# Cached attention beside a gated MLP, one token: MLP products behind the first K units, a longer loop on PE, and a re-ordered last head

## The chip, the cores and the metric

The kernel runs on one core of one Trainium2 chip. Its time is the device time of one execution in microseconds; three runs gave 2554.81, 2555.20 and 2555.25 us, a median of 2555.2. The engines are named PE (matrix products), DVE (vector), ACT (activation), POOL and SP (which issues the loads here). One execution was also recorded by the profiler.

## The reference

One token x (512 values) goes two ways, and a gate mixes them:

```python
g = sigmoid((x * gate_w).sum(-1, keepdims=True))
q = (x @ wq).reshape(B, Sq, H, Dh).transpose(0, 2, 1, 3)       # H = 32, Dh = 128
scores = einsum("bhqd,bhkd->bhqk", q, k_cache) * Dh ** -0.5    # Sk = 65536
o = einsum("bhqk,bhkd->bhqd", softmax(scores), v_cache)
a = o.transpose(0, 2, 1, 3).reshape(B, Sq, H * Dh) @ wo        # 512 columns
b = (silu(x @ w_gate) * (x @ w_up)) @ w_down                   # F = 1792
out = g * a + (1 - g) * b
```

All inputs are bf16. K and V of one head have 65536 rows of 128 values, 16.8 MB each; over 32 heads the two caches make up nearly all the bytes that are read.

## The kernel before

**Places and the order of loads.** SBUF holds a ring of four places (NPL = 4) of 4 MB. K and V of a head are four places each: k(h,0) to k(h,3), v(h,0) to v(h,3). `plan_stream` (L25) writes out the order of the loads: first wq, k(0,0), w_gate with w_up, w_down, then the other seven K places of heads 0 and 1; then, for heads 2 to 31, k(h,t) and v(h-2,t) in turn ("steady", 240 places); then the V places of heads 30 and 31 ("last"). Load number n goes to place n modulo 4. wo (4 MB) is loaded behind v(30,3) into kt, the buffer of transposed K, once all scores are done. The last place of all, v(31,3), is loaded in three parts of 64, 32 and 32 rows (L73), with a semaphore for each.

**SP** (L170 to L193) issues these loads strictly in order on one queue. Before a load that takes over a place it waits until the former owner has been read: a K place until DVE has transposed it (`ktdone`), a V place until its products are done (`pvdone`), wq until q is computed (`s_q`), w_gate and w_up until their products are done (`s_h`), w_down until its products are done (`s_b`). So k(0,3) takes the place of w_gate and w_up, and k(1,0) that of w_down.

**DVE** (from L264) transposes each K place in two units of 64 rows (L326), u = 0 to 7 in a head, into two buffers in turn; a unit's buffer is free again when the scores of the unit two before it are done. Between the units it does the small steps: the row maximum of the head before (L305), the transpose of its exponentials (L311), the reciprocal of its sum (L315), and, behind unit 4 of head 0, `mlp_steps` (L293 to L301): it waits for the exponential of the gate products (`s_sig`), makes silu(gate) * up (`s_gu`), then waits for the down products (`s_b`) and scales that row.

**PE** (from L347) computes q (L358). `scores(h, t)` (L385) makes 16 products with 512 moving columns for each unit (L396). In head 0, behind unit 3, come the 112 gate and up products (`mlp_up`, L373), and behind unit 4 the 14 down products (`mlp_down`, L381). `values(h, t)` (L406) multiplies a V place with the probabilities: for heads 0 to 30 in 32 products with V moving, 512 columns each, which sum four rows of 512 in psO (L418); for head 31 in 128 products with V stationary and one moving column, which sum one column of 128 (L423). For the former ACT scales the four rows by the reciprocal of the sum (`row_norm`, L225 to L230, into orow), PE turns them into one column with four products (`turn`, L429, L434, float32), and ACT copies the column (`column`, L232 to L234, into oTn). `turn(h-1)` stands behind v(h,1). `project(h)` (L438, L443) adds one head's column times wo to psY.

The order of PE's instructions is the order of the places. The K places of heads 0 and 1 and the first 20 steady places are written out, the next 208 are 13 passes of a hardware loop of 16 places (two heads; every wait shifts by 16 counts a pass), the last 12 steady places and the "last" ones are written out again. Behind v(31,2) PE waits for wo and does 31 wo products (L474 to L476), then v(31,3), and at last `project(31)`.

**The end.** DVE scales the column of head 31 out of psO (L340), PE does project(31), DVE mixes in the MLP row (L343), ACT stores the result (L260).

Of the kernel before, what the change touches and what calls it, by code (L numbers as in the profile page):

```python
# [6 lines left out]
ROWS = 128  # L7
# [3 lines left out]
NPL = 4  # L11
NSEM = 16
STEP = 8

ALU = mybir.AluOpType
ACT = mybir.ActivationFunctionType
# [19 lines left out]
def bass_gated_mix__mha_block_cached__swiglu_ffn__decode_kernel(  # L36
# [30 lines left out]
    for n, item in enumerate(items):  # L67
        s = n % NPL
        if item[0] in "kv":
            place[item] = s  # L70
            parts = [(0, ROWS)]
            if item == ("v", H - 1, PL - 1):
                parts = [(0, 64), (64, 96), (96, 128)]  # L73
            for r0, r1 in parts:
                landed[item + (r1,)] = len(dmas)
                dmas.append((item, r0, r1, s, owner[s]))
        else:
            for j, name in enumerate(item):
                place[name] = (s, j)
                landed[name] = len(dmas)  # L80
                dmas.append(((name,), 0, 0, s, owner[s]))
        owner[s] = item
        if item == ("v", H - 2, PL - 1):
            landed["wo"] = len(dmas)
            dmas.append((("wo",), 0, 0, None, None))

    with ExitStack() as ctx:
# [127 lines left out]
        @block.scalar  # L215
        def _(act):
            act.wait_ge(s_z, 1)
            nc.scalar.activation(sc[0:1, 1:2], sc[0:1, 0:1], ACT.Exp, scale=-1.0).then_inc(s_e1, 1)

            def windows(h):  # L220
                if h >= 2:
                    act.wait_ge(qkdone, UN * (h - 1))
                nc.scalar.copy(qcol[:, h % 2], qd[:, h, :, :]).then_inc(s_qw, STEP)  # L223

            def row_norm(h):  # L225
                act.wait_ge(s_li, h + 1)
                act.wait_ge(pvdone, PL * (h + 1))
                if h >= 1:
                    act.wait_ge(s_pt, h)
                nc.scalar.mul(orow[0:4, :], psO[0:4, h % 2, :], Li[0:4, h:h + 1]).then_inc(s_or, STEP)  # L230

            def column(h):  # L232
                act.wait_ge(s_pt, h + 1)
                nc.scalar.copy(oTn[:, h:h + 1], psT[:, h % 2:h % 2 + 1]).then_inc(s_oc, STEP)  # L234

            act.wait_ge(s_qd, 1)
            act.wait_ge(s_qz, 1)
            windows(0)
            windows(1)
            act.wait_ge(s_h, 1)  # L240
            nc.scalar.activation(hbuf[:, 0, 0:FC], psM[:, 64:64 + FC], ACT.Exp, scale=-1.0).then_inc(s_sig, 1)
            for h in range(H):
                act.wait_ge(s_ar, h + 1)
                nc.scalar.mul(nbias[:, h:h + 1], amx[:, h:h + 1], -SCALE).then_inc(s_nb, 1)  # L244
                act.wait_ge(s_nb, h + 1)
                if h >= 2:
                    act.wait_ge(s_pb, STEP * (h - 1))
                nc.scalar.activation(pa[:, h % 2, :], psS[:, h % 2, :], ACT.Exp, bias=nbias[:, h:h + 1],  # L248
                                     scale=SCALE, accum_out=rsum[:, h:h + 1]).then_inc(expdone, STEP)
                if h + 2 < H:  # L250
                    windows(h + 2)
                if h >= 3:
                    column(h - 3)
                if h >= 2:
                    row_norm(h - 2)
            column(H - 3)
            row_norm(H - 2)
            column(H - 2)
            act.wait_ge(s_fin, 1)
            act.dma_start(out_dram, fin[0:1, :]).then_inc(s_out, 16)  # L260
            act.wait_ge(s_out, 16)

        @block.vector
        def _(dve):  # L264
            chain = [0]

            def link(ins):
# [8 lines left out]
            nc.vector.tensor_tensor_reduce(out=orow[0:1, :], in0=xrow[0:1, :], in1=gwrow[0:1, :],  # L276
                                           scale=1.0, scalar=0.0, op0=ALU.mult, op1=ALU.add,
                                           accum_out=sc[0:1, 0:1]).then_inc(s_z, 1)
            dve.wait_ge(s_xT, 1)
            nc.vector.tensor_copy(xTb[:, 0:Dc], psM[:, 0:Dc]).then_inc(s_xTb, 1)  # L280
            dve.wait_ge(s_e1, 1)
# [11 lines left out]
            def mlp_steps():  # L293
                dve.wait_ge(s_sig, 1)
                link(nc.vector.tensor_scalar_add(hbuf[:, 1, 0:FC], hbuf[:, 0, 0:FC], 1.0))
                link(nc.vector.reciprocal(hbuf[:, 2, 0:FC], hbuf[:, 1, 0:FC]))
                link(nc.vector.tensor_tensor(hbuf[:, 0, 0:FC], psM[:, 64:64 + FC], hbuf[:, 2, 0:FC], ALU.mult))
                nc.vector.tensor_tensor(guT[:, 0:FC], hbuf[:, 0, 0:FC], psM[:, 80:80 + FC],
                                        ALU.mult).then_inc(s_gu, 1)
                dve.wait_ge(s_b, 1)  # L300
                link(nc.vector.tensor_scalar(brow[0:1, :], psY[0:1, :], sc[0:1, 4:5], None, ALU.mult))  # L301

# [14 lines left out]
            for h in range(H):  # L317
                for u in range(UN):
# [5 lines left out]
                    src = ring[:, place[("k", h, u // 2)], (u % 2) * UNIT:(u % 2 + 1) * UNIT]  # L324
                    src = src.bitcast(U32).rearrange("p (r j t) -> p r j t", j=2, t=32)
                    nc.vector.transpose(o, src).then_inc(ktdone, 1)  # L326
                    if i == 4:
                        mlp_steps()
                    if u == 0 and h >= 1:
                        head_max(h - 1)  # L330
                    if u == 1 and h >= 1:
                        head_turn(h - 1)
                    if u == 3 and h >= 1:
# [3 lines left out]
            head_norm(H - 1)  # L337
            dve.wait_ge(s_li, H)
            dve.wait_ge(pvdone, PL * H)
            nc.vector.tensor_scalar(oTn[:, H - 1:H], psO[:, (H - 1) % 2, 0:1], Li[:, H - 1:H], None,  # L340
                                    ALU.mult).then_inc(s_otn, 1)
            dve.wait_ge(s_y, 1)
            nc.vector.scalar_tensor_tensor(out=fin[0:1, :], in0=psY[0:1, :], scalar=sc[0:1, 3:4],  # L343
# [3 lines left out]
        def _(pe):  # L347
# [37 lines left out]
            def scores(h, t, more=0):  # L385
                for u in (2 * t, 2 * t + 1):
# [11 lines left out]
                                                    start=(u == 0 and k == 0 and je == 0),  # L398
                                                    stop=(u == UN - 1 and k == 3 and je == 3))
                    done.then_inc(qkdone, 1)  # L400
                    if h == 0 and u == 3:
                        mlp_up()
                    if h == 0 and u == 4:
                        mlp_down()

            def values(h, t, more=0):  # L406
                if t == 0:
                    pe.wait_ge(s_pb, STEP * (h + 1) + more)
                    if h >= 2:
                        pe.wait_ge(s_or, STEP * (h - 1) + more)  # L410
                v = ring[:, place[("v", h, t)], :]
                ends = [e for e in (64, 96, 128) if ("v", h, t, e) in landed]
                for r in range(0, ROWS, 4):
                    if r == 0 or r in ends:
                        arrived(pe, landed[("v", h, t, min(e for e in ends if e > r))], more)
                    k, rho = 8 * t + r // 16, r % 16
                    if h < H - 1:
                        done = nc.tensor.matmul(psO[0:4, h % 2, :], pbk[:, h % 2, k, rho:rho + 4],  # L418
                                                v[:, r * Dh:(r + 4) * Dh],
                                                start=(t == 0 and r == 0), stop=(t == PL - 1 and r == ROWS - 4))  # L420
                    else:
                        for j in range(4):
                            done = nc.tensor.matmul(psO[:, h % 2, 0:1], v[:, (r + j) * Dh:(r + j + 1) * Dh],  # L423
                                                    pbk[:, h % 2, k, rho + j:rho + j + 1],
                                                    start=(t == 0 and r + j == 0),
                                                    stop=(t == PL - 1 and r + j == ROWS - 1))
                done.then_inc(pvdone, 1)

            def turn(h, more=0):  # L429
                pe.wait_ge(s_or, STEP * (h + 1) + more)  # L430
                if h >= 2:
                    pe.wait_ge(s_oc, STEP * (h - 1) + more)
                for i in range(4):
                    done = nc.tensor.matmul(psT[:, h % 2:h % 2 + 1], orow[0:4, i * Dh:(i + 1) * Dh],  # L434
                                            unit[0:4, i:i + 1], start=(i == 0), stop=(i == 3))
                done.then_inc(s_pt, 1)

            def project(h):  # L438
                if h < H - 1:
                    pe.wait_ge(s_oc, STEP * (H - 1))  # L440
                else:
                    pe.wait_ge(s_otn, 1)
                done = nc.tensor.matmul(psY[0:1, :], oTn[:, h:h + 1], wo_ap[:, h, :],  # L443
# [4 lines left out]
            def run(item, more=0):  # L448
# [2 lines left out]
                    scores(h, t, more)  # L451
                else:
                    values(h, t, more)
                    if t == 1 and h >= 1:
                        turn(h - 1, more)

            pe.wait_ge(s_qd, 1)
            pe.wait_ge(s_unit, 1)
            head, per = 4 + 4 * PL, 4 * PL
            loops = (len(steady) - head) // per  # L460
            for item in first:
                if item[0] == "k":
                    run(item)
            for item in steady[:head]:
                run(item)
            with pe.Fori(0, STEP * 2 * loops, STEP * 2) as more:
                for item in steady[head:head + per]:
                    run(item, more)
            for item in steady[head + per * loops:]:
                run(item)  # L470
            for item in last:
                run(item)
                if item == ("v", H - 1, PL - 2):
                    arrived(pe, landed["wo"])  # L474
                    for h in range(H - 1):
                        project(h)  # L476
            project(H - 1)


# [26 lines left out]
```

## Time and profile before

| what | value |
|---|---|
| median of three runs | 2555.2 us |
| the profiled execution | 2555.05 us |
| its span (first to last instruction) | 2553.3 us |
| bytes read | 1087.64 MB, 426 GB/s over the span |
| PE busy | 2042.0 us (80%) |
| DVE busy | 1168.7 us (46%) |
| ACT, POOL busy | 56.1 us (2%), 26.0 us (1%) |
| transpose of one K unit (L326) | 4426 ns, 256 times |
| granted PE clock, mean | 0.90 |

The profiled execution's time is 1.75 us longer than its span. Busy time of an engine is the time in which its instructions run, waits left out; the products of PE overlap, so that 32 of them with a mean of 379 ns (L418) take 7.07 us together. The page cuts the span into 40 slices of 63.8 us and gives for each the busy tenths, the granted clock and the rate of the transfers.

### The profile page before, as it was taken

What the parts mean: (1) busy time and instruction counts of PE and PEld (TensorE: products, weight loads), DVE (VectorE), ACT (ScalarE), POOL (GpSimd) and SP (SyncE); (2) the same over time, 40 slices, a digit from 0 to 9 for tenths busy, and PEclk for the clock granted to TensorE, in tenths of its full rate; (3) what the DMA queues carried; (4) which work ended last, traced back from release to release, by engine and by line L of the source; (5) the groups of instructions that cost most, each with busy time, mean ns of one, the idle gap of its engine ahead of it and who ended that gap; (6) DMA issues with size and microseconds to landing.
All of it is one profiled execution on the core that took longest, in us unless ns stands there. A gap on an engine that the chain in (4) does not pass through costs nothing.

```text
span 2553.3 us, 19880 instructions
## 1 busy us (share of the span) xinstructions
PE 2042.0 (80%) x8992; PEld 824.2 (32%) x9118; DVE 1168.7 (46%) x373; ACT 56.1 (2%) x193; POOL 26.0 (1%) x75
## 2 busy tenths in 40 slices
PE   4778887887788788878877888887888788888885
PEld 2323333333333333333333333333333333333333
DVE  4754445444544544444454445445444544454420
ACT  0000000000000000000000000000000000000000
POOL 0000000000000000000000000000000000000000
PEclk8899889889988988899889988989888988899996
DMA  8999999999999999999999999999999999999998
GB/s 350 402 434 430 431 431 431 433 431 432 433 430 432 432 432 432 431 433 431 431 432 431 432 432 432 431 431 433 431 432 432 432 431 431 432 432 431 430 429 326
DMA packets 41879, 1088.11 MB, mean 426 GB/s; under 512 B 4211, under 2 KB 8310, under 8 KB 8310
## 3 DMA queue, kind: packets, MB, share of 16 engines
q1 hardware_dynamic: 41844, 1087.65, 99.2%
q8 instruction: 22, 0.36, 0.1%
q14 instruction: 11, 0.09, 0.0%
q10 hardware_dynamic: 2, 0.00, 0.0%
HBM read 1087.64 MB, written 0.00 MB: 426 GB/s over the span
## 4 chain that ended last, share of the span: by engine, by line
DMA 75%; DVE 12%; issue 10%; PE 2%; SPq 0%; DVEq 0%
DMA ring<-in_A_k_cache_dram 72%; DVE kt L326 12%; DMA ring<-in_A_v_cache_dram 3%; PE psS L396 1%; DMA gwrow<-in_gate_w_dram 0%; PE psY L443 0%; SPq L190 0%; PE psO L418 0%; PE psO L423 0%; PE psM L373 0%; PE psM L358 0%; PE psY L381 0%; DVE orow L276 0%; DVE brow L301 0%; DVE fin L343 0%
## 5 line engine op out<-in xcount | busy, mean ns | idle before, releaser
L326 DVE STREAM_TRANSPOSE kt<-ring 128x4096 uint32<-128x4096 uint32 x256 | 1125.6, 4426 | 1255.5 <-DMA ring<-in_A_k_cache_dram 1252.6
L396 PE MATMUL psS<-kt,qw 128*128 128x512 bf16 x3970 | 1104.3, 442 | 463.8 <-DVE kt L326 463.2
L418 PE MATMUL psO<-ring,pb 128*4 128x512 bf16 x3968 | 876.8, 379 | 5.0 <-DMA ring<-in_A_v_cache_dram 5.0
L396 PEld LDWEIGHTS psS<-kt,qw 128*128 128x128 bf16 x4096 | 429.7, 108 | 1124.3 <-issue 388.4
L418 PEld LDWEIGHTS psO<-ring,pb 128*4 128x4 bf16 x3968 | 335.2, 87 | 538.9 <-issue 53.2
L244 ACT ACTIVATE nbias<-amx 128x1 f32<-128x1 f32 x32 | 6.5, 203 | 2338.6 <-POOL amx L211 2338.6
L340 DVE TENSOR_SCALAR oTn<-psO,Li 128x1 bf16<-128x1 f32 x1 | 0.2, 220 | 83.8 <-PE psO L423 83.8
L211 POOL PARTITION_ALL_REDUCE amx<-mxs x32 | 11.2, 351 | 2383.9 <-DVE mxs L305 2383.9
L434 PEld LDWEIGHTS psT<-unit,orow 4*128 4x128 f32 x248 | 30.7, 190 | 13.1 <-issue 13.0
L423 PE MATMUL psO<-pb,ring 128*128 128x1 bf16 x512 | 14.1, 165 | 24.9 <-DMA ring<-in_A_v_cache_dram 24.9
L434 PE MATMUL psT<-unit,orow 4*128 4x1 f32 x248 | 33.3, 251 | 0.0
L311 DVE STREAM_TRANSPOSE pb<-pa 128x512 bf16<-128x512 bf16 x32 | 21.4, 670 | 6.4 <-PE psO L418 6.4
L305 DVE TENSOR_REDUCE mxs<-psS 128x1 f32<-128x512 f32 x32 | 20.9, 653 | 5.8 <-PE psS L396 5.8
L423 PEld LDWEIGHTS psO<-pb,ring 128*128 128x128 bf16 x512 | 13.8, 102 | 26.0 <-issue 15.4
L248 ACT ACTIVATE pa<-psS,nbias 128x512 bf16<-128x512 f32 x32 | 22.0, 687 | 2.9 <-ACT nbias L244 0.4
L230 ACT ACTIVATE orow<-psO,Li 4x512 f32<-4x512 f32 x31 | 20.9, 674 | 23.2 <-PE psO L418 23.2
L213 POOL PARTITION_ALL_REDUCE Lt<-rsum x32 | 12.3, 384 | 38.3 <-ACT pa L248 38.3
L352 PE MATMUL psM<-ones,xrow 1*128 1x1 bf16 x4 | 0.3, 172 | 13.9 <-DMA gwrow<-in_gate_w_dram 13.9
L443 PE MATMUL psY<-kt,oTn 128*1 128x512 bf16 x32 | 10.3, 492 | 0.4 <-DVE oTn L340 0.4
L223 ACT COPY qw<-qd 128x16 bf16<-128x16 bf16 x32 | 7.9, 250 | 6.0 <-DVE qd L289 6.0
L373 PEld LDWEIGHTS psM<-xTb,ring 128*128 128x128 bf16 x112 | 6.9, 159 | 0.2
L373 PE MATMUL psM<-xTb,ring 128*128 128x1 bf16 x112 | 6.8, 198 | 0.0
(39 smaller groups left out, 41.1 us busy)
## 6 DMA issues: line engine op xcount, KB each, us to landing
ring<-in_A_k_cache_dram SPq DMA_DIRECT2D x128, 4096.0 KB, 30.0
ring<-in_A_v_cache_dram SPq DMA_DIRECT2D x127, 4096.0 KB, 28.0
ring<-in_A_wq_dram SPq DMA_DIRECT2D x1, 4096.0 KB, 13.0
kt<-in_A_wo_dram SPq DMA_DIRECT2D x1, 4096.0 KB, 38.4
ring<-in_A_v_cache_dram SPq DMA_DIRECT2D x1, 2048.0 KB, 38.7
ring<-in_A_v_cache_dram SPq DMA_DIRECT2D x2, 1024.0 KB, 41.6
ring<-in_B_w_gate_dram SPq DMA_DIRECT2D x1, 1792.0 KB, 25.9
ring<-in_B_w_up_dram SPq DMA_DIRECT2D x1, 1792.0 KB, 29.6
```

What stands on the lines that cost most here:

```text
L211: nc.gpsimd.partition_all_reduce(amx[:, h:h + 1], mxs[:, h:h + 1], P, RMAX).then_inc(s_ar, 1)
L213: nc.gpsimd.partition_all_reduce(Lt[:, h:h + 1], rsum[:, h:h + 1], P, RADD).then_inc(s_L, 1)
L230: nc.scalar.mul(orow[0:4, :], psO[0:4, h % 2, :], Li[0:4, h:h + 1]).then_inc(s_or, STEP)
L248: nc.scalar.activation(pa[:, h % 2, :], psS[:, h % 2, :], ACT.Exp, bias=nbias[:, h:h + 1], scale=SCALE, accum_out=rsum[:, h:h + 1]).then_i ...
L305: nc.vector.reduce_max(mxs[:, h:h + 1], psS[:, h % 2, :], AX_X).then_inc(s_mx, 1)
L311: nc.vector.transpose(pb[:, h % 2, :], pa[:, h % 2, :]).then_inc(s_pb, STEP)
L326: nc.vector.transpose(o, src).then_inc(ktdone, 1)
L373: done = nc.tensor.matmul(psM[:, o + j:o + j + 1], w[:, c, :, j], xTb[:, c:c + 1], start=(c == 0), stop=(c == Dc - 1))
L396: done = nc.tensor.matmul(psS[:, h % 2, :], qw[:, h % 2, je, at0:at0 + 128], ktb[i % 2][:, je // 2, k, :, je % 2], start=(u == 0 and k == ...
L418: done = nc.tensor.matmul(psO[0:4, h % 2, :], pbk[:, h % 2, k, rho:rho + 4], v[:, r * Dh:(r + 4) * Dh], start=(t == 0 and r == 0), stop=(t ...
L423: done = nc.tensor.matmul(psO[:, h % 2, 0:1], v[:, (r + j) * Dh:(r + j + 1) * Dh], pbk[:, h % 2, k, rho + j:rho + j + 1], start=(t == 0 an ...
L434: done = nc.tensor.matmul(psT[:, h % 2:h % 2 + 1], orow[0:4, i * Dh:(i + 1) * Dh], unit[0:4, i:i + 1], start=(i == 0), stop=(i == 3))
```

## The change

- The MLP's gate and up products move from behind unit 3 of head 0 to behind unit 0, the down products from behind unit 4 to behind unit 1. On DVE `mlp_steps` moves from behind unit 4 to behind unit 1, and its last step is a function of its own, `mlp_row`, behind unit 3.
- PE's loop takes all 240 steady places in 15 passes. So that each pass is alike, the waits on `s_or` and `s_oc` have no exceptions for the first heads; instead DVE sets orow to zero at the start and counts `s_or` up by two heads, ACT counts `s_oc` up by three, and a turn of "head -1" is done behind v(0,1).
- Head 31 uses the products with V moving in its first three places. ACT copies their four rows unscaled, `turn(31)` brings them as a column into psT in front of v(31,3), and the 128 one-column products of v(31,3) add to that column. DVE scales it at the end.
- v(31,3) is loaded in four parts: 64, 32, 16 and 16 rows.
- The wo products of heads 0 to 29 stand behind v(31,0), that of head 30 behind v(31,1).

```diff
+ENDS = (64, 96, 112, 128)
...
-                parts = [(0, 64), (64, 96), (96, 128)]
+                parts = [(a, b) for a, b in zip((0,) + ENDS, ENDS)]
...
             def row_norm(h):
...
-                if h >= 1:
-                    act.wait_ge(s_pt, h)
+                act.wait_ge(s_pt, h + 1)
...
             def column(h):
-                act.wait_ge(s_pt, h + 1)
+                act.wait_ge(s_pt, h + 2)
...
+            act.sem_inc(s_oc, 3 * STEP)
...
             column(H - 2)
+            act.wait_ge(pvdone, PL * H - 1)
+            nc.scalar.copy(orow[0:4, :], psO[0:4, (H - 1) % 2, :]).then_inc(s_or, STEP)
...
+            dve.wait_ge(s_z, 1)
+            nc.vector.memset(orow[:], 0.0).then_inc(s_or, 2 * STEP)
...
+            def mlp_row():
                 dve.wait_ge(s_b, 1)
...
-                    if i == 4:
+                    if i == 1:
                         mlp_steps()
+                    if i == 3:
+                        mlp_row()
...
-            nc.vector.tensor_scalar(oTn[:, H - 1:H], psO[:, (H - 1) % 2, 0:1], Li[:, H - 1:H], None,
+            nc.vector.tensor_scalar(oTn[:, H - 1:H], psT[:, (H - 1) % 2:(H - 1) % 2 + 1], Li[:, H - 1:H], None,
...
-                    if h == 0 and u == 3:
+                    if h == 0 and u == 0:
                         mlp_up()
-                    if h == 0 and u == 4:
+                    if h == 0 and u == 1:
                         mlp_down()
...
-                    if h >= 2:
-                        pe.wait_ge(s_or, STEP * (h - 1) + more)
+                    pe.wait_ge(s_or, STEP * (h + 1) + more)
...
-                    if h < H - 1:
+                    if (h, t) != (H - 1, PL - 1):
...
-                            done = nc.tensor.matmul(psO[:, h % 2, 0:1], v[:, (r + j) * Dh:(r + j + 1) * Dh],
+                            done = nc.tensor.matmul(psT[:, h % 2:h % 2 + 1], v[:, (r + j) * Dh:(r + j + 1) * Dh],
...
             def turn(h, more=0):
-                pe.wait_ge(s_or, STEP * (h + 1) + more)
-                if h >= 2:
-                    pe.wait_ge(s_oc, STEP * (h - 1) + more)
+                pe.wait_ge(s_or, STEP * (h + 3) + more)
+                pe.wait_ge(s_oc, STEP * (h + 2) + more)
...
-                    pe.wait_ge(s_oc, STEP * (H - 1))
+                    pe.wait_ge(s_oc, STEP * (h + 4))
...
-                    if t == 1 and h >= 1:
+                    if t == 1:
                         turn(h - 1, more)
...
-            with pe.Fori(0, STEP * 2 * loops, STEP * 2) as more:
-                for item in steady[head:head + per]:
+            with pe.Fori(0, STEP * 2 * (len(steady) // per), STEP * 2) as more:
+                for item in steady[:per]:
                     run(item, more)
...
+                if item == ("v", H - 1, PL - 1):
+                    turn(H - 1)
                 run(item)
-                if item == ("v", H - 1, PL - 2):
+                if item == ("v", H - 1, 0):
                     arrived(pe, landed["wo"])
-                    for h in range(H - 1):
+                    for h in range(H - 2):
                         project(h)
+                if item == ("v", H - 1, 1):
+                    project(H - 2)
             project(H - 1)
```

## The prediction

> **What bounds the kernel now.** I read the page's slices first: is any stretch not bound by transfers?
>
> ```profile
> DMA  8999999999999999999999999999999999999998
> GB/s 350 402 434 430 431 431 431 433 431 432 433 430 432 432 432 432 431 433 431 431 432 431 432 432 432 431 431 433 431 432 432 432 431 431 432 432 431 430 429 326
> ```
>
> From the third slice to the last but one the DMA engines are full at about 432 GB/s, and the page's first line has 1088.11 MB in all: at 432 that is 2518.8 us of the 2553.3 us span. So 34.5 us are missing from the stream, nearly all in the first two slices and the last (a little in the transfer of wo). PE is busy 80%, DVE 46%; in the middle a faster engine buys nothing. The change must be priced at the two ends.
>
> At the start, the view by stretches of 4 us shows the gap (columns: stretch, length, busy time and instructions of each engine, granted PE clock, DMA share, GB/s):
>
> ```profile
> 48.00:52.00 4.00, 1.12 (x3) 0.42 (x4) 4.00 (x2) 0.00 (x0) 0.00 (x0) 0.50 1.07 459
> 52.00:56.00 4.00, 4.00 (x14) 1.49 (x13) 3.14 (x1) 0.00 (x0) 0.00 (x0) 0.69 0.44 188
> 56.00:60.00 4.00, 3.94 (x22) 1.84 (x21) 3.56 (x1) 0.00 (x0) 0.00 (x0) 1.00 0.02 4
> 60.00:64.00 4.00, 4.00 (x70) 4.00 (x69) 0.89 (x1) 0.00 (x0) 0.00 (x0) 1.00 0.00 0
> 64.00:68.00 4.00, 3.75 (x47) 3.04 (x48) 0.76 (x4) 0.18 (x1) 0.00 (x0) 0.59 0.39 106
> 68.00:72.00 4.00, 4.00 (x11) 1.38 (x10) 0.00 (x0) 0.00 (x0) 0.00 (x0) 0.56 0.73 311
> ```
>
> The queue is empty from about 54.5 to 67. Why, say the waits of SP's queue in the first 130 us:
>
> ```profile
> SPq L190 <- PE psM L373: 33.7, 1, 33.7
> SPq L190 <- PE psY L381: 8.8, 1, 8.8
> ```
>
> SP issues in order. After k(0,2) at about 32.6 it stands 33.7 us at the load of k(0,3), whose slot holds w_gate and w_up until the MLP's first products (L373, s_h) end at 66.6; meanwhile everything issued lands. It then waits for the down products (L381, s_b) to load k(1,0).
>
> At the end, the timeline:
>
> ```profile
> 2514.07 3.56 PE L423 MATMUL psO<-pb,ring 128*128 128x1 bf16 x128 [14.51 <-DMA ring<-in_A_v_cache_dram]
> 2533.43 3.57 PE L423 MATMUL psO<-pb,ring 128*128 128x1 bf16 x128 [4.36 <-DMA ring<-in_A_v_cache_dram]
> 2536.93 9.73 PE L443 MATMUL psY<-kt,oTn 128*1 128x512 bf16 x31
> 2546.59 3.37 PE L423 MATMUL psO<-pb,ring 128*128 128x1 bf16 x128
> 2550.07 0.22 DVE L340 TENSOR_SCALAR oTn<-psO,Li 128x1 bf16<-128x1 f32 x1 [83.75 <-PE psO L423]
> ```
>
> PE waits for the first place of the last V, but the last place starts without a wait: 31 wo products stand before it. In stretches of 1 us the last bytes land at about 2542.7, so here PE sets the end, 4 us behind the data.
>
> **Start: MLP products earlier.** Unit 0 of k(0,0) is transposed at 28.4 and its 16 products start at 28.88; twelve run 0.427 us apart, four 0.221: 6.0 us, to 34.9. wg and wu were issued at 2.20 and 2.73 and take 25.9 and 29.6 us (DMA issues), so they are there at 32.3. L373 took 6.83 us: s_h at 41.8 instead of 66.6. k(0,1) lands at 46.4 and k(0,2) near 54.5, so k(0,3) is queued 12 us before the queue would run dry. Unit 1: 16 products, 3.5 (all at 0.221) to 6.8 us (all at 0.427); L381 has 14: 3.18 us as recorded, 6.0 at 0.427. s_b is thus at 48.5 to 54.6. k(0,3) would land at about 64 (9.71 us a place), so k(1,0) also comes 9 us before it is needed. The next load, k(1,1), needs k(0,1) transposed: two times 4.4 us behind 46.4, 55.2, again early.
>
> Price: the stretch 52 to 88 moved 264 GB/s, 36 x 264/432 = 22.0 us worth; **14.0 us** of stream are missing and come back. Lower bound 12.0, the empty windows 55 to 67 alone; nothing if a new wait takes their place (below). The first 52 us (414 GB/s) lack another 2.1 us at launch, which stays. From there the stream runs full, so whatever is gained at 88 us is still gained at v(31,0)'s landing.
>
> The DVE edits: mlp_steps after unit 1 waits from 32.6 to about 42 for s_sig; behind it stands unit 2, whose data comes at 46.4, so its cover is 4 us. mlp_row after unit 3 (55.2) finds s_b done; 0.74 us (L301), and DVE has nearly 2 us of slack per head in the K-only stretch (38.85 us of stream for four places of 8.86 and about 1.5 of small steps). The new memset of orow goes in front of the cast at 14.56: qw's 640 words took 0.59 us, so 512 take about 0.5, and wq's products, s_q and the load of k(0,1) are 0.6 us later (19.0 instead of 18.36). The queue holds work until about 37, so nothing; without that cover 0.6.
>
> **Middle: the loop.** Thirty heads go through PE's loop instead of 26 (32 unrolled places go). PE's wait constants shift together with the extra start counts on s_or and s_oc, so each wait asks for the same event as before; added is turn(-1), 1.05 us (L434) once, inside PE's waits of about 3.8 us per K place. Fewer instructions are fetched: q8 moved 22 packets of 16 KB, 13 before 480 us and 9 after 2300, none between. By the code about half of PE's written-out instructions go; if q8 is theirs, half of 0.36 MB, 0.4 us of stream. But the K period is 38.85 us with a packet in it and without one. I take 0.2; bounds 0 and 0.8 (all of q8).
>
> A rule speaks against loops. The Trainium skill (Runtime: NRT & Kernel Launch, Instruction fetch mechanics) says that a taken branch out of the prefetched window stalls for a fetch, though it gives PE room for 2048 instructions. The trace has no q8 packet during thirteen passes, and PE's waits at the pass boundaries are those on DVE that all places have. By the rule two more passes add two stalls, under PE's slack: nothing in the sum either way.
>
> **End: PE's work after v(31,0) lands**, in the old time base (all landings shift alike). Start 2514.07.
> - v(31,0), now 32 moving products: 7.0 us warm (L418: 7.07 with its tail). PE has idled 14.5 us and its clock is 0.50 by then. Six bursts of 512-wide products that began cold (28.88, 50.88, 66.86, 81.04, 2448.78, 2536.93) had 12, 9, 11, 10, 12 and 14 products 0.427 apart: 11.3 x 0.206 = 2.3 us more. To 2523.4. Bounds: 0 to 3.3 (16 cold).
> - 30 wo products at 0.227 (3.18/14): 6.8, to 2530.2. wo landed near 2504.
> - v(31,1), landed at 2523.7: 7.0, to 2537.2. turn(30) 1.05, then the ACT column (0.09 + 0.16 + 0.1) and one product 0.23: 2538.8.
> - v(31,2), landed at 2533.4: 7.0, to 2545.8. ACT copies psO: 0.18 to start and 0.68 (as at 2499.74), 0.06 to PE: 2546.7.
> - turn(31) 1.05, then v(31,3) as before, 128 products, 3.4: 2551.2.
>
> Before it was 2549.96, so the tail is **1.3 us longer** (-1.0 to +2.3). The steps behind it (L340, L443, L343, the store) are unchanged. What was late in the old tail, the wo products, is hidden, but three places cost twice PE's time; PE, not the last landing, still sets the end, and so the fourth part of the last place (16 rows) is worth nothing.
>
> On the clock, the Trainium skill (TensorE: Matmul & The Clock Gate, Part 1) gives about 3.4 us until full speed; the bursts here took 3.7 to 5.9. By the page eight products would be cold, 1.6 us, and the time 0.7 less.
>
> **Sum.** -14.0 + 1.3 - 0.2 = -12.9 on the profiled execution's 2555.05 (0.15 under the median): **2542.2**. By the bounds: 2555.05 - 14.0 - 1.0 - 0.8 = 2539.2, and 2555.05 - 12.0 + 2.3 = 2545.4.
>
> **Rivals.**
> - *A new gap.* PE stands in the MLP early and unit 2 comes late, so a slot is released late and the queue runs dry again. For: SP is strictly in order, four gates follow each other. Against: margins of 9 us and more at each. It costs what it misses; with 4 to 8 us lost, 2546 to 2550.
> - *Nothing gained.* The change doesn't do what it says because a third release gates SP over the same stretch (psS or the DVE chain behind the MLP): about 2555. Against: SP's list of waits has no other long one in the first 130 us.
> - *Slower: the clock stays half in the tail.* For: it was 0.50 from 2502 to 2542 though PE ran 384 products. Against: those were one-column products with idle time between; every 512-wide burst brought it up within 6 us. Price: three places of 13.7, 31 products of 0.427, two turns of 1.87, 0.36 and 0.92 of waits, 3.56: 62.9 us, to 2577.0, 27.0 late; 2555.05 - 14.2 + 27.0 = 2567.9. It outweighs the gain once some 74 of the tail's 127 wide products are cold (11 assumed, 12.9/0.206 = 63 more).
>
> **Chances.** Forecast (2539.2 to 2545.4) 0.82; new gap 0.09; nothing gained 0.05; clock 0.04. A measurement here can tell about 0.2%, 5 us. The first two are faster by more: 0.91; the third the same: 0.05; the last slower: 0.04. The range, 2539.2 to 2547.5, holds the forecast and the start of the new gap.
>
> **What would show it.** Right: the first two slices near 418 and 432 GB/s; SP's wait on L373 about 9 us instead of 33.7; 4064 moving products (now L418) and 128 one-column ones (now L423); no PE wait in front of v(31,1) and v(31,2); and about 8.5 us, not 7.3, from the last V landing to the end of v(31,3)'s products. Wrong: an empty stretch of the queue elsewhere before 130 us, products 0.427 apart beyond the first dozen of the last head, or a period other than 38.85 us in the middle.

## The result, and the profile after

The changed kernel takes 2542.47 us (median of five runs, 2541.93 to 2542.85) where the kernel before took 2555.25 beside it: a ratio of 0.9949, 95% interval 0.9934 to 0.9963. The forecast was 2542.2. Its profiled execution took 2542.47 us with a span of 2540.6, 12.7 us less than before.

The slices of the page, changed kernel:

```profile
DMA  9999999999999999999999999999999999999997
GB/s 414 431 432 430 432 431 433 431 431 434 430 431 433 432 430 433 431 430 432 434 430 431 434 431 431 434 430 431 433 432 430 434 431 430 433 432 431 432 425 317
```

The first two slices stand at 414 and 431 GB/s instead of 350 and 402; the last one is as low as it was. The gain is at the start. The stretches that were empty (same columns as before: the last three are PE clock, DMA share, GB/s):

```profile
52.00:56.00 4.00, 3.46 (x16) 1.34 (x15) 4.00 (x2) 0.00 (x0) 0.00 (x0) 1.00 0.97 418
56.00:60.00 4.00, 3.33 (x15) 1.25 (x13) 3.62 (x2) 0.00 (x0) 0.00 (x0) 1.00 0.95 410
60.00:64.00 4.00, 2.94 (x13) 1.27 (x14) 4.00 (x2) 0.00 (x0) 0.00 (x0) 1.00 1.07 459
64.00:68.00 4.00, 3.47 (x16) 1.37 (x15) 3.12 (x2) 0.00 (x0) 0.00 (x0) 1.00 1.03 438
```

SP's waits in the first 130 us show the cause: it stood 33.7 us at w_gate's place, now 8.5.

```profile
SPq L191 <- PE psM L383: 8.5, 1, 8.5
SPq L191 <- PE psY L391: 7.7, 1, 7.7
```

At the end, the timeline of PE (start, length, line, products; in brackets the wait in front and what ended it):

```profile
2500.80 9.41 PE L427 MATMUL psO<-ring,pb 128*4 128x512 bf16 x32 [14.12 <-DMA ring<-in_A_v_cache_dram]
2510.04 6.64 PE L450 MATMUL psY<-kt,oTn 128*1 128x512 bf16 x30
2516.52 7.07 PE L427 MATMUL psO<-ring,pb 128*4 128x512 bf16 x32
2523.52 1.05 PE L441 MATMUL psT<-unit,orow 4*128 4x1 f32 x8
2524.87 0.38 PE L450 MATMUL psY<-kt,oTn 128*1 128x512 bf16 x1 [0.31 <-ACT oTn L234]
2525.09 7.07 PE L427 MATMUL psO<-ring,pb 128*4 128x512 bf16 x32
2532.88 1.05 PE L441 MATMUL psT<-unit,orow 4*128 4x1 f32 x8 [0.72 <-ACT orow L262]
2533.86 3.41 PE L432 MATMUL psT<-pb,ring 128*128 128x1 bf16 x128
```

PE waits for v(31,0) and for no later place. It starts on v(31,3) at 2533.86, while the last bytes land by 2529.4 (in stretches of 0.2 us). So PE still sets the end, 7.9 us from the last landing to the last V product; read the same way it was 7.4 before (2542.6 to 2549.96).

### The profile page after: what moved, and what is told of

Read it like the earlier page. It is cut to its first block, busy times and chain, and to the rows that moved or that the text cites. A ratio compares the mean times of both kernels' runs of the same rounds, so it can differ in the third digit from the quotient of the medians.

```text
span 2540.6 us, 19360 instructions
## 1 busy us (share of the span) xinstructions
PE 2046.1 (81%) x8734; PEld 819.6 (32%) x8846; DVE 1169.2 (46%) x374; ACT 56.8 (2%) x194; POOL 26.1 (1%) x75
## 5 line engine op out<-in xcount | busy, mean ns | idle before, releaser
L427 PE MATMUL psO<-ring,pb 128*4 128x512 bf16 x4064 | 902.2, 380 | 19.4 <-DMA ring<-in_A_v_cache_dram 19.4
L427 PEld LDWEIGHTS psO<-ring,pb 128*4 128x4 bf16 x4064 | 344.5, 87 | 568.8 <-issue 73.9
L313 DVE TENSOR_REDUCE mxs<-psS 128x1 f32<-128x512 f32 x32 | 20.9, 653 | 3.9 <-PE psS L406 3.9
L230 ACT ACTIVATE orow<-psO,Li 4x512 f32<-4x512 f32 x31 | 20.9, 675 | 21.6 <-PE psO L427 21.6
```

The lines of the kernel that those rows point to most:

```text
L313: nc.vector.reduce_max(mxs[:, h:h + 1], psS[:, h % 2, :], AX_X).then_inc(s_mx, 1)
```

## Experiments

Two theories. **Gap**: the whole gain is the queue's empty stretch at the start; the new last head costs a little. **End**: a good part of the gain comes from taking the wo products off the last place. Each kernel was timed in five runs (`tail_alone`, `loop_alone` and `up_u2` in eleven) beside the kernel before, and each ratio is to those runs. Where two changed kernels are compared, their medians come mostly from separate series; the medians of the kernel before in these series lie between 2554.93 and 2555.79, so a difference under 1 us between two changed kernels says little.

### One part alone

`mlp_alone`, on the kernel before:

```diff
+            def mlp_row():
...
-                    if i == 4:
+                    if i == 1:
                         mlp_steps()
+                    if i == 3:
+                        mlp_row()
...
-                    if h == 0 and u == 3:
+                    if h == 0 and u == 0:
                         mlp_up()
-                    if h == 0 and u == 4:
+                    if h == 0 and u == 1:
                         mlp_down()
```

> The kernel before with the MLP edits alone (products behind units 0 and 1, steps on DVE behind units 1 and 3); loop and end as before. Theory 'gap': the whole gain is the queue's empty stretch at the start, so the time falls by 13 to 14 us, to 2541 to 2542, a little below the full change; the end keeps its 35.9 us from v(31,0)'s first product to the last V product. Rival 'end': a good part of the gain came from moving the wo products off the last place; then the MLP edits alone give only 6 to 9 us, 2546 to 2549.

Measured 2541.39 us, ratio 0.9944 (0.9930 to 0.9957). The start alone gives all of it; "end" falls: the changed kernel's last head adds nothing to that gain.

`tail_alone`, on the changed kernel (the MLP's four places and the loop put back as they were):

```diff
-                    if h == 0 and u == 0:
+                    if h == 0 and u == 3:
                         mlp_up()
...
-                for item in steady[:per]:
+                for item in steady[head:head + per]:
...
```

> The changed kernel with the MLP products back behind units 3 and 4 and the loop of 13 passes; so the last head's edits alone (with the zeroed row and the start counts). Theory 'gap': the tail is 0.6 us longer, as in the changed kernel's trace (36.45 us against 35.9 from v(31,0)'s first product to the last V product), so 2555 to 2557. Rival 'end': 2548 to 2551.

Measured 2556.97 us, ratio 1.0007 (0.9998 to 1.0016). The last head's edits gain nothing. In its trace 36.5 us pass from v(31,0)'s first product (2515.07) to the last V product, 0.6 more than before, and v(31,0) starts 1.0 us later than before; 0.6 us of that is there already when k(0,3) is issued (67.25 instead of 66.65). The end of the interval leaves "no change" open.

`loop_alone`, on the changed kernel: the MLP put back as above, the last head as in `stat_early` below with its wo products and three parts as before. What stays of the change is the loop and what makes its passes alike. Against the kernel before:

```diff
-            with pe.Fori(0, STEP * 2 * loops, STEP * 2) as more:
-                for item in steady[head:head + per]:
+            with pe.Fori(0, STEP * 2 * (len(steady) // per), STEP * 2) as more:
+                for item in steady[:per]:
                     run(item, more)
```

> The changed kernel with the MLP products and the last head as before: all 30 steady heads in PE's loop, alone. Theory: the one long K period of 20.9 us at about 383 us in the trace of before is where PE enters its loop, and goes (1.4 us); fewer fetches give nothing else: 2553.5 to 2555.5. Rival: the loop costs fetch stalls: over 2556.

Measured 2555.66 us, ratio 1.0001 (0.9992 to 1.0010): no change. The 1.4 us that I had read into one long K period were not found as a gain; the trace has no 20.9 us period, but one of 20.35 at 150 us and four more of 20.4 behind it. The premise was wrong, too: by the order of the places PE's loop in the kernel before begins with k(4,2), which DVE transposes from 323 us, not at 383. The rival's stall isn't seen either: the median lies inside the spread of the kernel before (2553.3 to 2557.2), though the interval leaves a cost of up to 2.6 us open.

### How late may the MLP be

`up_u1` on the changed kernel (`up_u2` has units 2 and 3 in these lines, and DVE's two steps behind units 3 and 5):

```diff
-                    if h == 0 and u == 0:
+                    if h == 0 and u == 1:
                         mlp_up()
-                    if h == 0 and u == 1:
+                    if h == 0 and u == 2:
                         mlp_down()
```

> The changed kernel with the gate and up products behind unit 1 and the down products behind unit 2 (the step on DVE stays where it is): w_gate's place is released at about 45.5 us instead of 42.0, w_down's at 60 to 63 instead of 50. Theory 'gap': the queue runs dry only at about 55 and, with k(0,3) in it, at about 66; both loads still come in time and nothing changes: 2541 to 2543.5. Rival: a later release costs what it is late, 3.5 us and more: 2546 to 2552.

Measured 2542.41 us, ratio 0.9946 (0.9933 to 0.9960): nothing lost, though SP's wait on the gate and up products grew from 8.5 to 12.4 us and that on the down products from 7.7 to 14.1.

> The changed kernel with the gate and up products behind unit 2, the down products behind unit 3, DVE's steps behind units 3 and 5. Theory 'gap': unit 2 is only transposed at 51.2 us, its products end near 57 (half clock), the gate and up products near 64, and k(0,3) is issued then, 9 us after the queue ran dry and 2.5 us earlier than in the kernel before: most of the gain is lost, 2551 to 2555. Rival: the gain is PE's earlier work as such, not the queue; then one unit later costs little more than behind unit 1: 2543 to 2546.

Measured 2553.58 us, ratio 0.9990 (0.9981 to 0.9999). One unit later and the gap is back, in the stretches of `up_u2`:

```profile
52.00:56.00 4.00, 4.00 (x13) 1.51 (x12) 3.42 (x1) 0.00 (x0) 0.00 (x0) 0.64 0.46 197
56.00:60.00 4.00, 4.00 (x62) 3.73 (x61) 0.00 (x0) 0.00 (x0) 0.00 (x0) 1.00 0.02 4
60.00:64.00 4.00, 4.00 (x58) 3.45 (x58) 0.38 (x2) 0.18 (x1) 0.00 (x0) 0.71 0.00 0
64.00:68.00 4.00, 4.00 (x11) 1.45 (x10) 3.93 (x4) 0.00 (x0) 0.00 (x0) 0.50 1.08 385
```

SP's wait there is 30.1 us, and k(0,3) is issued at 63.36 (expected near 64). The issue of k(0,3) and the transpose of head 2's first place, in the kernel before, the changed kernel, `up_u1` and `up_u2`:

```profile
66.65 0.33 SPq L190 DMA_DIRECT2D ring<-in_A_k_cache_dram  x1
41.98 0.33 SPq L191 DMA_DIRECT2D ring<-in_A_k_cache_dram  x1
45.54 0.33 SPq L191 DMA_DIRECT2D ring<-in_A_k_cache_dram  x1
63.36 0.33 SPq L191 DMA_DIRECT2D ring<-in_A_k_cache_dram  x1
128.83 4.44 DVE L326 STREAM_TRANSPOSE kt<-ring 128x4096 uint32<-128x4096 uint32 x1 [0.94 <-DMA ring<-in_A_k_cache_dram]
114.76 4.45 DVE L334 STREAM_TRANSPOSE kt<-ring 128x4096 uint32<-128x4096 uint32 x1 [0.93 <-DMA ring<-in_A_k_cache_dram]
114.71 4.45 DVE L334 STREAM_TRANSPOSE kt<-ring 128x4096 uint32<-128x4096 uint32 x1 [0.66 <-DMA ring<-in_A_k_cache_dram]
125.68 4.45 DVE L334 STREAM_TRANSPOSE kt<-ring 128x4096 uint32<-128x4096 uint32 x1 [0.94 <-DMA ring<-in_A_k_cache_dram]
```

Issued 3.6 us later than in the changed kernel, k(0,3) costs head 2 nothing; 21.4 us later it costs head 2 10.9 us. From `up_u2` to the kernel before it is 3.3 us later once more, and head 2 begins 3.15 us later. So a late release is free until the queue runs dry, and from there on nearly every microsecond counts.

### The clock in the tail

`warm60`, on the changed kernel (added work whose result nothing reads):

```diff
+                if item == ("v", H - 2, PL - 1):
+                    for _ in range(60):
+                        nc.tensor.matmul(psM[0:4, :], sel[:, 0, 0:4], pb[:, 0, :], start=True, stop=True)
```

> The changed kernel with 60 added products of 512 moving columns between v(30,3) and v(31,0), into a PSUM tile that nothing reads any more: about 13 us of PE work in a wait of 14.1 us, so that the clock is full when v(31,0) lands. Theory: the 2.3 us in the tail's sum for a cold start are real and on the path, since PE has a backlog from there to the end: v(31,0) takes 7.07 us instead of 9.41 and the time falls by 2.3 us against the changed kernel, to 2539.5 to 2541. Rival: the tail is bound by the landings; then 2542 to 2543.

Measured 2540.34 us, ratio 0.9940 (0.9926 to 0.9953), 2.1 us below the changed kernel. Its timeline:

```profile
2486.97 13.11 PE L479 MATMUL psM<-pb,sel 128*4 128x512 bf16 x60
2501.17 7.07 PE L427 MATMUL psO<-ring,pb 128*4 128x512 bf16 x32 [1.09 <-DMA ring<-in_A_v_cache_dram]
2508.07 6.64 PE L450 MATMUL psY<-kt,oTn 128*1 128x512 bf16 x30
```

v(31,0) takes 7.07 us instead of 9.41: the cold start costs 2.34 us, and nearly all of it was on the path. From v(31,0)'s first product to the last V product 34.1 us pass instead of 36.5. That work which nothing needs makes the kernel faster shows that PE's backlog, not the landings, sets the end.

### V stationary or moving, wo products early or late

`stat_early`, on the changed kernel: head 31 as in the kernel before in all four places, the wo products where the change has them.

```diff
-                    if (h, t) != (H - 1, PL - 1):
+                    if h < H - 1:
...
-                            done = nc.tensor.matmul(psT[:, h % 2:h % 2 + 1], v[:, (r + j) * Dh:(r + j + 1) * Dh],
+                            done = nc.tensor.matmul(psO[:, h % 2, 0:1], v[:, (r + j) * Dh:(r + j + 1) * Dh],
...
-                if item == ("v", H - 1, PL - 1):
-                    turn(H - 1)
...
```

> The changed kernel with the last head's V stationary in all four places as in the kernel before (128 one-column products of 3.5 us a place, no turn(31), no copy), the wo products staying behind v(31,0) and v(31,1). Theory: PE's backlog sets the end, and its cause is the three places of 7 us; with 3.5 us each PE has no backlog when the last part lands, and the last V product ends within 1 us of the last landing instead of 7.5 us behind it: 2534.5 to 2536.5. Rival: the wo products at half clock (30 x 0.427 = 12.8 us) keep PE behind all the same: 2540 to 2543.

Measured 2535.55 us (2535.50 to 2535.82), ratio 0.9921 (0.9907 to 0.9935): the fastest of all, 6.9 us below the changed kernel. Its timeline:

```profile
2513.09 3.39 PE L430 MATMUL psO<-pb,ring 128*128 128x1 bf16 x128
2519.97 3.57 PE L430 MATMUL psO<-pb,ring 128*128 128x1 bf16 x128 [0.80 <-DMA ring<-in_A_v_cache_dram]
2528.58 0.58 PE L430 MATMUL psO<-pb,ring 128*128 128x1 bf16 x16 [0.20 <-DMA ring<-in_A_v_cache_dram]
2529.79 0.59 PE L430 MATMUL psO<-pb,ring 128*128 128x1 bf16 x16 [0.62 <-DMA ring<-in_A_v_cache_dram]
2530.48 0.22 DVE L348 TENSOR_SCALAR oTn<-psO,Li 128x1 bf16<-128x1 f32 x1 [77.39 <-PE psO L430]
```

v(31,1) still starts without a wait, behind the 30 wo products (9.06 us, from 2504.10), but v(31,2) and the last parts of v(31,3) wait for their data, and 0.6 us of products are left behind the last landing.

`mov_late`, on the changed kernel:

```diff
-                if item == ("v", H - 1, 0):
+                if item == ("v", H - 1, PL - 2):
                     arrived(pe, landed["wo"])
-                    for h in range(H - 2):
+                    for h in range(H - 1):
                         project(h)
-                if item == ("v", H - 1, 1):
-                    project(H - 2)
```

> The changed kernel with all 31 wo products behind v(31,2), as in the kernel before, and the last head's V moving in three places as in the change: the fourth corner of (V moving or stationary) x (wo products late or early). Theory: PE's work between v(31,0)'s landing and the last V product is a backlog. With moving V, 9.4 us for v(31,0) and 7.0 for each of the next two go between landings 9.7 us apart with little left over, then 31 wo products of 0.216 (6.7 us), turn(31) and the last place follow: about 1 us longer than the changed kernel, 2543 to 2545. Rival: the wo products' place alone makes the difference, as it does with stationary V (6 us): 2547 to 2549.

Measured 2545.15 us, ratio 0.9959 (0.9946 to 0.9973), 2.7 us above the changed kernel, where about 1 was expected, and 0.15 above the expected range. Its timeline has most of the surplus in the clock, 1.54 us: PE waits 1.68 us in front of v(31,2), and that place (at 2520.10) then takes 8.61 us instead of 7.07. The first two lines, from v(30,1) and v(30,2), are taken up at the end.

```profile
2466.95 1.05 PE L441 MATMUL psT<-unit,orow 4*128 4x1 f32 x8
2469.66 7.07 PE L427 MATMUL psO<-ring,pb 128*4 128x512 bf16 x32 [1.66 <-DMA ring<-in_A_v_cache_dram]
2517.37 1.05 PE L441 MATMUL psT<-unit,orow 4*128 4x1 f32 x8
2520.10 8.61 PE L427 MATMUL psO<-ring,pb 128*4 128x512 bf16 x32 [1.68 <-DMA ring<-in_A_v_cache_dram]
```

The four corners, with the MLP early in each (the first is `mlp_alone`, which has the old loop and three parts, too):

| | wo products late | wo products early |
|---|---|---|
| V stationary | 2541.39 | 2535.55 |
| V moving | 2545.15 | 2542.47 |

Moving the wo products is worth 5.8 us with stationary V and 2.7 with moving V; the moving V costs 3.8 and 6.9. The change joined a gain to a larger cost.

### The parts of the last place

`after_parts1` (changed kernel) and `stat_parts1` (`stat_early`): v(31,3) in one piece.

```diff
-ENDS = (64, 96, 112, 128)
+ENDS = (128,)
```

> The changed kernel with the last V place loaded in one piece instead of four. Theory: PE reaches v(31,3) 4 us after its last bytes have landed, so the parts are worth nothing in this kernel: 2541 to 2543.5. Rival: the parts matter: 2544 to 2546.

Measured 2542.83 us, ratio 0.9947 (0.9934 to 0.9961): the same as with four parts.

> stat_early with the last V place loaded in one piece. Theory: where PE has no backlog, the last place's 128 one-column products (3.5 us) all stand behind the last landing, where they were 0.6 us for the last 16 rows: about 2.9 us longer than stat_early, 2537.5 to 2539.5. The same edit was worth nothing in the changed kernel. Rival: the pieces only cost issue time: 2535 to 2536.

Measured 2538.80 us, ratio 0.9936 (0.9922 to 0.9949), 3.25 us above `stat_early`. The same edit is worth nothing where PE has a backlog and about 3 us where it has none.

## Why the prediction was right, point by point

**The gap.** Its mechanism stands: SP's wait, the empty stretches, and `up_u1` with no loss beside `up_u2` with most of it agree with it. s_h was forecast for 41.8 and s_b for 48.5 to 54.6; in the trace the gate and up products end at 41.96 and the down products at 49.97. The new memset made the load of k(0,1) 0.85 us later (19.21 instead of 18.36), not 0.6; the queue held work as forecast, and no empty stretch came of it. The size, 14.0 us, is right at the start: the transpose of the first place of head 2 begins at 114.76 instead of 128.83, 14.07 us earlier. v(31,0), however, starts 13.27 us earlier (2500.80 against 2514.07), where the sum had 14.2. So the sentence that whatever is gained at 88 us is still gained at the end did not hold in these two traces, by 0.8 us. The stream isn't quite even: some K places come 0.95 us late. In DVE's timeline of the changed kernel:

```profile
600.88 8.77 DVE L334 STREAM_TRANSPOSE kt<-ring 128x4096 uint32<-128x4096 uint32 x2 [9.48 <-DMA ring<-in_A_k_cache_dram]
621.26 8.77 DVE L334 STREAM_TRANSPOSE kt<-ring 128x4096 uint32<-128x4096 uint32 x2 [11.57 <-DMA ring<-in_A_k_cache_dram]
640.70 8.77 DVE L334 STREAM_TRANSPOSE kt<-ring 128x4096 uint32<-128x4096 uint32 x2 [10.66 <-DMA ring<-in_A_k_cache_dram]
```

One period is 20.38 us, the next 19.44. The changed kernel's trace has four such periods (at 621, 1127, 1614 and 2120 us), together 3.8 us; that of the kernel before has three long ones, 20.92 at 383, 20.23 at 1646 and 20.39 at 2152, together some 3.2 us. So they carry a part of the 0.8 us, not all of it. They may come with the longer loop: all nine traces of kernels that have it show the four, while of the three without it `mlp_alone` shows three of them, the kernel before the last two and `tail_alone` none (but one of 20.96 at 424). One trace of each kernel can't tell that from chance, the runs of one kernel spread over 0.3 to 3.7 us, and `loop_alone` shows no cost beyond its interval; the cause stays open. A period other than 38.85 us (two K places in the middle) was one of the prediction's signs of being wrong. It did appear, but already in the kernel before, where the prediction had overlooked it.

**The tail.** Forecast 37.1 us from v(31,0)'s first product to the last V product, measured 36.5; before it was 35.9. The cold start was right (9.24 us to the next product against 9.3). Mis-sized were the 30 wo products, 6.48 us at 0.216 instead of 6.8 at 0.227 (a mean of 14 that carries the end of the last one), and some tenths in the waits for ACT: the copy of orow took 0.58 us, not 0.68. So the tail costs 0.6 us, not 1.3, and the last V product ends 7.9 us behind the last landing, not 8.5.

**The two misses offset each other**: 0.9 us too much at the start, 0.7 too much at the end. The forecast's 0.3 us from the median is partly luck; its terms are good to a microsecond.

**The loop.** Forecast 0.2 us, measured nothing that can be told apart (1.0001, 0.9992 to 1.0010). q8 moved 11 packets instead of 22 (20 in `tail_alone`, 13 in `loop_alone`, so it follows the loop). Eight come up to 248 us, the last four of them in the first of the fifteen passes, which begins with k(2,0) at 114.76 and takes some 155 us; none comes in the fourteen passes behind it. In the kernel before it was alike: the prediction found no packet during the thirteen passes, but four, near 344, 381, 417 and 456 us, fall into the first one. The Trainium skill (Runtime: NRT & Kernel Launch, Instruction fetch mechanics) lets a branch out of the prefetched window stall for a fetch. From the second pass on the trace shows no fetch, and between 300 and 2300 us all waits of PE's products are put down to DVE; a stall inside these waits would not be seen. By the code a pass has some 530 products, each with a load of weights, so some 1,060 instructions besides the waits. That this fits the 2048 instructions which the same section gives PE is in agreement.

**The parts.** "Worth nothing" was right for this kernel, shown by `after_parts1`.

**The rivals.** A new gap: didn't come; `up_u1` and `up_u2` show between which releases it starts. Nothing gained: refuted by the result, and for the MLP edits alone by `mlp_alone`. The clock at half: the tail went back to full speed within v(31,0). The Trainium skill (TensorE: Matmul & The Clock Gate, Part 1) gives about 3.4 us until then. In the trace, 2.34 us lost at 0.206 a product are 11 products, 4.8 us. The measurement decides: nearer to the bursts of this trace than to the page.

## What to carry to other kernels

Where one engine issues all loads in order, look for the wait at which it stands while the queue runs dry; releasing that buffer earlier gained about the empty time here (14.07 us at head 2, 13.27 at the last head), and releasing it 3.6 us earlier still gained nothing. At the end of a stream ask whether PE or the last landing is late: with a backlog, PE's total work there counts (and waking its clock with useless products paid 2.1 us here), and finer last pieces were worth something only when the backlog was gone. Test the parts of a joint change in all combinations: here one half (V moving) hid a gain of 5.8 us of the other (wo products early).

## What was not expected of the hardware

- At the same places of the stream, 487 to 506 us apart, a K place comes 0.95 us late, in some traces and not in others (all nine with the longer loop). Each is preceded, by 5 to 16 us, by one 8 KB instruction packet on q14; there are such packets without a late place, too. No run here was made to tell the cause, and it stays open.
- A pause of 1.68 us with 1.05 us of one-column products ahead of it can be enough for the clock to fall: in `mov_late` it was granted 1.00 until 2518, 0.59 on average from 2520 to 2524. It need not: in the same trace a pause of 1.66 us behind the same products, in front of 2469.66, left it at 1.00, and the place behind it took 7.07 us. What decides between the two stays open.
- The last transfers thin out over some 3.5 us: in the changed kernel the stretch 2526 to 2528 moves 76 GB/s and 2528 to 2530 moves 18.
